# Chunks 2 and 3 of normalised x: 32x32 block turns on DVE and placement through DRAM in place of TensorE transposes

## The chip, the cores and the metric

The kernel runs on one core of one Trainium2 chip. The metric is the device time in microseconds (us) of one execution; lower is better. The engines are named as in the profile: PE (TensorE; PEld is its weight load), DVE (VectorE), ACT (ScalarE), POOL (GpSimd) and SP (SyncE, which here issues nearly all DMA transfers; SPq is its queue of issues).

## What is computed

One transformer-like block on 2048 tokens of width 576, in float32: layer norm without gain or bias, 32-head attention (head width 18), a bilinear GLU of width 4608, and a gated sum.

```python
xn = _layernorm(x, axis=-1)                    # x: [1, 2048, 576]
s = _A_ref(xn, A_wqkv, A_wo)                   # attention, 32 heads, output projection
g = _silu(_B_ref(xn, B_w_gate, B_w_up, B_w_down))   # ((xn @ w_gate) * (xn @ w_up)) @ w_down
return x + s * g
```

The three attention products q, k, v are xn @ wqkv with wqkv of [576, 1728].

## The kernel before

Every float32 product is computed as three products of split operands: a value is written as a high part (float32r, made by an ACT copy) and a low part (the difference, made by DVE or POOL). For normalised x the two parts lie in a tile `xc` of [128, 9, 512] for a chunk of 512 tokens: columns of x (576 of them) on the partitions, tokens along the free axis; slots 0 to 3 hold the high parts of columns 0 to 511, slots 4 to 7 their low parts, slot 8 the last 64 columns, high in partitions 0 to 63 and low in 64 to 127.

There are four chunks of 512 tokens (c = 0 to 3). The kernel has a prologue (about the first 195 us), which makes the columns of x and the q, k and v projections, and a main part, in which a planner interleaves attention with the GLU. The change lies in the prologue, whose order is written out by hand (L557 to L643) and kept on every engine as written.

What one chunk goes through in the prologue:

- `load_x` (L346) brings 512 rows of x into `xin` [128, 4, 576], four transfers of 128 rows, row on partition. There are two such buffers.
- `norm` (L378) runs `norm_stats` (DVE bn_stats twice and bn_aggr, then a square root on ACT, L360) and `norm_apply` (DVE reciprocal, DVE (x - mean) * r into `xn`, L369, and a copy of the last 64 columns beside themselves, L374 on DVE, so that the fifth transpose fills 128 partitions). It is called for two 128-row groups at a time. `xn` has one buffer.
- `to_columns` (L386) turns `xn` with PE: 20 transposes of 128x128 into five PSUM banks (L401). ACT copies each bank into the high slot (L404, L408), DVE subtracts for the low slot (L405, L409). Chunk 0 has its own form, `first_columns`.
- `qk_block` (L458) computes 128 of the 1152 columns of q and k for the chunk's 512 tokens: 14 matmuls of 128x128 by 128x512 (L463) in a bank that is taken in turn from four ("a" and "b", two each). ACT and DVE split the result into `hl` (L466, L467; three buffers), and SP stores it to `sqk` in DRAM (L473; 512 KB in one or two transfers).
- `x_store` (L538) stores `xc` of chunks 1 to 3 to `sx` in DRAM, for the GLU.
- `v_block` (L515) computes v for 128 tokens: two groups of 14 matmuls of 128x128 by 128x288 (L520), in two of the four "g" banks; ACT empties them (L526), SP stores the rows to `sv` (L528). `v_fetch` and `v_split` (L495, L504) load and split the weights of v, in two halves.
- `w_fetch` (L535) loads weights of q and k for two blocks, six transfers (L111, L114).

The loop over chunks:

```python
    for c in range(NCH):
        if c + 2 < NCH:
            load_x(c + 2)
        for b in range(3):
            qk_block(b, c)
        ...
        if c + 1 < NCH:
            to_columns(c + 1)
        for b in range(3, 6):
            qk_block(b, c)
        ...
            if b < 5 and c + 2 < NCH:
                norm(c + 2, (0, 1) if b == 3 else (2, 3))
            if c in (1, 2):
                x_store(c, range(3 * (b - 3), 3 * (b - 2)))
```

So chunk c + 1 is turned between blocks 2 and 3 of chunk c, and chunk c + 2 is normalised while blocks 3 to 5 of chunk c run. With c = 1 there follow, before chunk 2's first block, `w_fetch(3)` and the four v blocks of chunk 0 (called v0 to v3 below), then `w_fetch(4)`. With c = 0 the second half of v's weights is fetched after block 5 (L587).

Each engine works through its instructions in the order in which this code emits them, and so does SP with its DMA issues: an issue whose data is not ready holds back all issues behind it. SP's transfers use eight semaphores in turn, and an issue also waits until the transfer eight before it has landed.

Functions that the diff touches, and what calls them:

Of the kernel before, what the change touches and what calls it, by code (L numbers as in the profile page):

```python
# [20 lines left out]
FT = mybir.dt.float32  # L21
FR = mybir.dt.float32r
I32 = mybir.dt.int32
AF = mybir.ActivationFunctionType
OP = mybir.AluOpType
# [16 lines left out]
def kernel(  # L42
# [10 lines left out]
    nc = tc.nc  # L53
    _, S, D = x.shape
# [5 lines left out]
    NCH = S // 512  # L60
# [6 lines left out]
    dram = ctx.enter_context(tc.tile_pool(name="dram", bufs=1, space=bass.MemoryType.DRAM))  # L67
    consts = ctx.enter_context(tc.tile_pool(name="consts", bufs=1))
    wpool = ctx.enter_context(tc.tile_pool(name="wpool", bufs=1))
    xcp = ctx.enter_context(tc.tile_pool(name="xcp", bufs=2))  # L70
# [6 lines left out]
    sv = dram.tile([S, H, DH + 1], FT, name="sv")  # L77
    sot = dram.tile([D, S], FT, name="sot")
    sg = dram.tile([S, D], FT, name="sg")
    swo = dram.tile([128, 10, D], FT, name="swo")  # L80

    turns = [0]

    def bank(tag, bufs, k=None):
        if tag == "g":
            if k is None:
                k = turns[0] = (turns[0] + 1) % 4
            return psum.tile([128, 512], FT, name="pg", tag=f"g{k}", bufs=1)
        return psum.tile([128, 512], FT, name="p" + tag, tag=tag, bufs=bufs)
# [6 lines left out]
    x2 = x.rearrange("o s d -> (o s) d")  # L96
# [10 lines left out]
    def w_load(srcs):  # L107

        raw = wpool.tile([128, 2, 5, 128], FT, name="wraw", bufs=2)[:, 0:len(srcs)]
        for i, (m, c0) in enumerate(srcs):  # L110
            nc.sync.dma_start(raw[:, i, 0:4, :],  # L111
                              m[0:512, c0:c0 + 128].rearrange("(k p) c -> p k c", p=128))
            for b in (0, 64):
                nc.sync.dma_start(raw[b:b + 64, i, 4, :], m[512:576, c0:c0 + 128])  # L114
        return raw
# [108 lines left out]
    graw, gw, draw, dw = {}, {}, {}, {}  # L224
# [100 lines left out]
    xcs = [None] * NCH  # L325
    vstack, pro = ExitStack(), ExitStack()
    vp = vstack.enter_context(tc.tile_pool(name="vp", bufs=1))
    pp = pro.enter_context(tc.tile_pool(name="pro", bufs=1))
# [15 lines left out]
    xin, xns = {}, {}  # L344

    def load_x(c):  # L346
        xin[c] = ep.tile([128, 4, D], FT, name="xin", bufs=2)
        for t in range(4):
            nc.sync.dma_start(xin[c][:, t, :], x2[c * 512 + t * 128:c * 512 + t * 128 + 128, :])

# [2 lines left out]
    def norm_stats(c, t):  # L353
        st = ep.tile([128, 2, 6], FT, name="st", bufs=4)
        mv = ep.tile([128, 2], FT, name="mv", bufs=4)
        rs = ep.tile([128, 2], FT, name="rs", bufs=4)
        for g in range(2):
            nc.vector.bn_stats(st[:, g, :], xin[c][:, t, g * HALF:(g + 1) * HALF])  # L358
        nc.vector.bn_aggr(mv, st)
        nc.scalar.activation(rs[:, 0:1], mv[:, 1:2], AF.Sqrt, bias=eps)  # L360
        stat[c, t] = mv, rs

    def norm_apply(c, t):
        if t == 0:
            xns[c] = ep.tile([128, 4, 640], FT, name="xn", bufs=1)
        xn = xns[c]
        mv, rs = stat.pop((c, t))
        nc.vector.reciprocal(rs[:, 1:2], rs[:, 0:1])
        op = nc.vector.tensor_scalar(xn[:, t, 0:D], xin[c][:, t, :], mv[:, 0:1], rs[:, 1:2],  # L369
                                     op0=OP.subtract, op1=OP.mult)  # L370
        if c < 2 and t == 3:
            behind.append(op)
        if c:
            nc.vector.tensor_copy(xn[:, t, D:640], xn[:, t, 512:D])  # L374
        else:
            nc.scalar.activation(xn[:, t, D:640], xn[:, t, 512:D], AF.Copy)

    def norm(c, ts=range(4)):  # L378
        for t in ts:
            norm_stats(c, t)  # L380
        for t in ts:
            norm_apply(c, t)

    nqk = [0]

    def to_columns(c):  # L386

        xn = xns.pop(c)
        if c < 2:
            xc = pp.tile([128, 9, 512], FR, name="xcx", bufs=2)  # L390
        else:
            xc = xcp.tile([128, 9, 512], FR, name="xc")
        xcs[c] = xc
        for k in range(5):
            if k < 4:
                p = bank("g", 3)
            else:
                p = bank("a" if nqk[0] % 2 else "b", 2)
                nqk[0] += 1
            for t in range(4):  # L400
                nc.tensor.transpose(p[:, t * 128:(t + 1) * 128],  # L401
                                    xn[:, t, k * 128:(k + 1) * 128], ident)
            if k < 4:
                nc.scalar.activation(xc[:, k, :], p, AF.Copy)  # L404
                nc.vector.tensor_tensor(xc[:, 4 + k, :], p, xc[:, k, :].bitcast(FT),  # L405
                                        op=OP.subtract)
            else:
                nc.scalar.activation(xc[:, 8, :], p, AF.Copy)  # L408
                nc.vector.tensor_tensor(xc[64:128, 8, :], p[64:128, :],  # L409
                                        xc[64:128, 8, :].bitcast(FT), op=OP.subtract)  # L410

    def first_columns():
# [15 lines left out]
        norm_stats(0, 0)  # L428
        norm_stats(0, 1)
        norm_apply(0, 0)  # L430
        norm_stats(0, 2)
        turn(0)
        warm(2)
        wq[0], todo = w_split(raws[0], 2)
        for f, a in todo[:2]:
            f(*a, rest=False)
        norm_apply(0, 1)
        norm_stats(0, 3)
        turn(1)
# [18 lines left out]
    def qk_block(b, c):  # L458
        w, ninth = (t[:, b % 2] for t in wq[b // 2])
        p = bank("a" if nqk[0] % 2 else "b", 2)  # L460
        nqk[0] += 1
        for n, (a, e) in enumerate(QK_PAIRS):
            nc.tensor.matmul(p, w[:, a, :] if a < 9 else ninth, xcs[c][:, e, :], start=n == 0,  # L463
                             stop=n == len(QK_PAIRS) - 1)
        hl = pp.tile([128, 2, 512], FR, name="hl", bufs=3)
        nc.scalar.activation(hl[:, 0, :], p, AF.Copy)  # L466
        nc.vector.tensor_tensor(hl[:, 1, :], p, hl[:, 0, :].bitcast(FT), op=OP.subtract)  # L467
        g0 = blocks[b]
        for kind in range(2):
            lo, hi = max(g0, kind * D), min(g0 + 128, (kind + 1) * D)  # L470
            if lo < hi:
                dst = sqk[kind, :, lo - kind * D:hi - kind * D, c * 512:(c + 1) * 512]
                nc.sync.dma_start(dst.rearrange("h r s -> r h s"), hl[lo - g0:hi - g0].bitcast(FT))  # L473
# [41 lines left out]
    def v_block(t):  # L515
        c, r = divmod(t, 4)
        ps = [bank("g", 3), bank("g", 3)]
        for h in range(2):
            for n, (a, e) in enumerate(PAIRS):
                nc.tensor.matmul(ps[h][:, 0:HALF], xcs[c][:, e, r * 128:(r + 1) * 128],  # L520
                                 vbox["w"][:, a, h * HALF:(h + 1) * HALF], start=n == 0,
                                 stop=n == len(PAIRS) - 1)
        v = vrows[vturn[0] % len(vrows)]
        vturn[0] += 1
        for h in range(2):
            nc.scalar.activation(v[:, 16 * h:16 * h + 16, 0:DH],  # L526
                                 ps[h][:, 0:HALF].rearrange("p (a b) -> p a b", b=DH), AF.Copy)
        nc.sync.dma_start(sv[t * 128:(t + 1) * 128], v)  # L528

    def w_now(i):  # L530
        wq[i], todo = w_split(raws[i], 1 if i == 4 else 2, ep if i == 2 else pp if i == 4 else None)
        for f, a in todo:
            f(*a)

    def w_fetch(i):  # L535
        raws[i] = w_load([(wqkv, b) for b in blocks[2 * i:2 * i + 2]])
# [19 lines left out]

    raws = {}  # L557
    load_x(0)
    w_fetch(0)
    load_x(1)  # L560
    w_fetch(1)
    first_columns()
# [4 lines left out]
# [4 lines that stand above are left out]
            qk_block(b, c)  # L571
            if c == 0 and b == 0:
                w_now(2)
        if c + 1 < NCH:
            to_columns(c + 1)
        for b in range(3, 6):
            qk_block(b, c)
            if c == 1 and b == 3:
                v_split(c)
            if b < 5 and c + 2 < NCH:  # L580
                norm(c + 2, (0, 1) if b == 3 else (2, 3))
            if c in (1, 2):
                x_store(c, range(3 * (b - 3), 3 * (b - 2)))
            if c == 0 and b == 3:
                v_split(c)
            if c == 0 and b == 5:
                v_fetch(1)  # L587
            if c == NCH - 1 and b == 3:
                w_now(3)
        if c == 1:  # L590
            w_fetch(3)
            for t in range(4):
                v_block(t)
            w_fetch(4)
        if c == 2:
            w_now(4)
# [780 lines left out]
    with ExitStack() as end:  # L1377
# [45 lines left out]
        for i, t in enumerate(order):  # L1423
# [13 lines left out]
            y = ys[i % 4]  # L1437
# [3 lines left out]
            xt = xi.pop(t)  # L1441
# [40 lines left out]
```

## Time and profile before

| | |
|---|---|
| time, median of 3 runs (lowest to highest) | 2592.74 us (2592.35 to 2594.34) |
| time of the profiled execution | 2593.44 us |
| its span, first to last instruction | 2591.3 us |
| granted TensorE clock | 1.000 |
| PE busy | 2582.0 us |
| DVE, ACT, POOL busy | 1813.5, 1550.6, 675.8 us |
| PE transposes of `to_columns` (L401) | 60 of 271 to 273 ns, from 21.5 to 82.0 us |
| first matmul of chunk 2's block 0 | 70.34 us |

The page gives the busy time of each engine, the chain of work that ended last (followed back from the last instruction to what released it), and the costliest groups of instructions. The timeline lists instructions in order of time, neighbours of one line merged: start, length, engine, line, operation, tiles, count, and in brackets how long the engine had been idle and for whom. A matmul's end is modelled and neighbours overlap, so the time from start to start is what one costs. DMA issues stand in the rows of SPq; how long a transfer took to land is seen in the chain of waits, where it has a row of its own.

### The profile page before, as it was taken

The numbers are of one execution on the slowest core, as the hardware profiler recorded it, in microseconds if no ns is written. First come the engines' busy times: TensorE is split into PE (matmuls) and PEld (weight loads), VectorE is DVE, ScalarE is ACT, GpSimd is POOL, SyncE is SP. The second block draws the span as 40 slices with busy tenths as digits, with TensorE's granted clock in tenths as the row PEclk, the third lists the DMA queues.
The fourth block names the chain that finished last, engine by engine and source line by source line (L and its number), as shares of the span: only waits on it lengthen the run. The fifth ranks groups of instructions, "written<-read, shape, count | busy, mean of one in ns | idle before, by whom it ended". The sixth has DMA issues, their size and how long they took to land.

```text
span 2591.3 us, 59623 instructions
## 1 busy us (share of the span) xinstructions
PE 2582.0 (100%) x24440; PEld 2132.3 (82%) x24440; DVE 1813.5 (70%) x2996; ACT 1550.6 (60%) x3096; POOL 675.8 (26%) x697
## 2 busy tenths in 40 slices
PE   9999999999999999999999999999999999999999
PEld 7899877888888888888878887777887877877889
DVE  7209777777777778777777877777777777777238
ACT  4223677766766666666666666666666666666621
POOL 3114444434431222222111222111111222221016
PEclk9999999999999999999999999999999999999999
DMA  7899767677653444454444443444444444443357
GB/s 243 251 299 260 202 184 194 184 193 212 175 190 114 142 163 135 151 161 160 142 168 149 142 140 127 138 145 159 121 158 124 145 150 141 133 140 112 124 204 252
DMA packets 186066, 435.65 MB, mean 168 GB/s; under 512 B 51041, under 2 KB 111105, under 8 KB 155585
## 3 DMA queue, kind: packets, MB, share of 16 engines
q1 hardware_dynamic: 183632, 423.88, 53.0%
q0 software_dynamic: 2160, 7.96, 0.8%
q8 instruction: 192, 3.15, 0.5%
q14 instruction: 82, 0.66, 0.1%
HBM read 315.16 MB, written 111.35 MB: 165 GB/s over the span
## 4 chain that ended last, share of the span: by engine, by line
PE 97%; DVE 1%; DMA 1%; ACT 0%; issue 0%; SPq 0%; ACTq 0%; DVEq 0%
PE pg L775 36%; PE pg L734 17%; PE pg L836 16%; PE pa L671 11%; PE pb L723 9%; PE pg L520 2%; PE pb L463 2%; PE pa L463 1%; PE pg L1431 1%; DMA sqk<-hl 1%; PE pb L1431 1%; PE pa L1431 1%; DVE st L358 0%; DMA wgu<-swg 0%; DVE xn L369 0%; PE pa L723 0%
## 5 line engine op out<-in xcount | busy, mean ns | idle before, releaser
L673 DVE TENSOR_REDUCE mx<-pa 128x1 f32<-128x512 f32 x2016 | 1348.8, 687 | 331.9 <-PE pa L671 156.3
L775 PE MATMUL pg<-xc,wgu 64*128 64x512 f32 x7776 | 1442.5, 392 | 0.4 <-DMA wgu<-swg 0.3
L725 ACT ACTIVATE pt<-pb 128x512 f32<-128x512 f32 x2005 | 1144.5, 602 | 471.3 <-PE pb L723 369.0
L775 PEld LDWEIGHTS pg<-xc,wgu 64*128 64x128 f32 x7776 | 1078.8, 186 | 45.5 <-issue 0.8
L836 PE MATMUL pg<-wd,hs 64*128 64x288 f32 x6816 | 877.7, 293 | 0.0
L836 PEld LDWEIGHTS pg<-wd,hs 64*128 64x128 f32 x6816 | 815.2, 185 | 11.6 <-issue 0.8
L671 PE MATMUL pa<-whole,turning 54*128 54x512 f32 x1999 | 783.2, 399 | 0.3 <-DVE mx L673 0.3
L723 PE MATMUL pb<-whole,turning 56*128 56x512 f32 x1978 | 775.2, 398 | 0.0
L734 PE MATMUL pg<-pt,vt 128*32 128x512 f32 x4096 | 453.3, 594 | 0.1
L671 PEld LDWEIGHTS pa<-whole,turning 54*128 54x128 f32 x1999 | 363.3, 184 | 75.3 <-issue 53.0
L816 POOL TENSOR_TENSOR hs<-us,hs 128x512 fp32r<-128x512 f32 x144 | 186.0, 1292 | 866.4 <-ACT hs L800 610.0
L863 POOL TENSOR_TENSOR acc<-acc,st 128x288 f32<-128x288 f32 x284 | 229.5, 810 | 606.0 <-ACT st L893 341.0
L723 PEld LDWEIGHTS pb<-whole,turning 56*128 56x128 f32 x1978 | 360.0, 184 | 5.7 <-ACT pt L725 0.2
L734 PEld LDWEIGHTS pg<-pt,vt 128*32 128x32 f32 x4096 | 126.2, 110 | 285.1 <-issue 279.2
L740 DVE TENSOR_TENSOR oc<-oc,pg 128x512 f32<-128x512 f32 x35 | 24.1, 688 | 221.2 <-PE pg L734 214.9
L257 POOL TENSOR_TENSOR wgu<-wraw,wgu 128x384 fp32r<-128x384 f32 x108 | 108.1, 1014 | 215.3 <-ACT wgu L256 97.6
L738 ACT ACTIVATE oc<-pg 128x512 f32<-128x512 f32 x32 | 19.1, 598 | 229.4 <-PE pg L734 222.0
L899 DVE TENSOR_TENSOR acc<-acc,pg 128x288 f32<-128x288 f32 x261 | 116.3, 448 | 38.5 <-PE pg L836 34.5
L792 DVE TENSOR_TENSOR us<-pg,us 128x512 f32<-128x512 f32 x144 | 98.6, 685 | 54.0 <-PE pg L775 50.9
L893 ACT ACTIVATE st<-pg 128x288 f32<-128x288 f32 x284 | 117.1, 413 | 27.0 <-PE pg L836 19.9
L785 ACT ACTIVATE us<-pg 128x512 f32<-128x512 f32 x143 | 85.5, 598 | 76.6 <-PE pg L775 65.4
L800 ACT ACTIVATE hs<-us 128x512 fp32r<-128x512 f32 x142 | 89.4, 630 | 15.9 <-DVE us L792 15.4
(154 smaller groups left out, 1288.8 us busy)
## 6 DMA issues: line engine op xcount, KB each, us to landing
wgu<-swg SPq DMA_DIRECT2D x102, 1152.0 KB
wd<-swd SPq DMA_DIRECT2D x50, 1152.0 KB
swg<-wgu SPq DMA_DIRECT2D x36, 1152.0 KB
whole<-sqk SPq DMA_DIRECT2D x192, 144.0 KB
turning<-sqk SPq DMA_DIRECT2D x384, 72.0 KB
swd<-wd SPq DMA_DIRECT2D x18, 1152.0 KB
sqk<-hl SPq DMA_DIRECT2D x32, 512.0 KB
xc<-sx SPq DMA_DIRECT2D x24, 512.0 KB
```

Source lines behind the costliest of these rows:

```text
L257: nc.gpsimd.tensor_tensor(w[:, 9 + b:12 + b, :], raw[:, b:b + 3, :], w[:, b:b + 3, :].bitcast(FT), op=OP.subtract)
L671: nc.tensor.matmul(p, q[rows, t * 128:(t + 1) * 128], k[rows, c * 512:(c + 1) * 512], start=True, stop=True)
L673: nc.vector.tensor_reduce(mx[h][:, t, c:c + 1], p, axis=AX.X, op=OP.max)
L723: nc.tensor.matmul(p, k[rows, t * 128:(t + 1) * 128], q[rows, c * 512:(c + 1) * 512], start=True, stop=True)
L725: nc.scalar.activation(pt[t, c // 2][:, c % 2, :], p, AF.Exp, scale=scale)
L734: nc.tensor.matmul(p[32 * c:32 * c + 32, :], vt[h // 2][:, t, 6 * (h % 2):6 * (h % 2) + 32], pt[t, c // 2][:, c % 2, :], start=t == ts[0], ...
L775: nc.tensor.matmul(ps, gw[n][half[r], a, :], xg[i][half[r], e, :], start=k == 0, stop=k == len(TERMS) - 1)
L816: nc.gpsimd.tensor_tensor(hj[:, 1, :], h32, hj[:, 0, :].bitcast(FT), op=OP.subtract)
L836: op = nc.tensor.matmul(ps[:, 0:HALF], hs[u][half[r], j, a, s * 128:(s + 1) * 128], dw[u][half[r], j, e, i * HALF:(i + 1) * HALF], start=( ...
L863: nc.gpsimd.tensor_tensor(a, a, st, op=OP.add)
L893: nc.scalar.activation(st, ps[:, 0:HALF], AF.Copy)
L899: nc.vector.tensor_tensor(a, a, ps[:, 0:HALF], op=OP.add)
```

## The change

For c = 2 and 3, `load_x` places the rows differently (token 128a + 32t + j of a chunk on partition 32a + j, slot t; four transfers that reach 32 partitions each). Once the chunk is normalised, `turn_blocks` turns `xn` in 32x32 blocks on DVE, four instructions of 128x576, back into the `xin` buffer. `blocks_out` stores this with four transfers (pieces of 512 bytes) to a new scratch tensor `sxt` in DRAM, where it lies as columns by tokens. `blocks_in` reads it back with three transfers (pieces of 2048 bytes; 1024 KB and two of 128 KB) into two tiles that use the places of `wd` and `draw`. `late_columns` splits it from SBUF: five ACT copies and five DVE subtractions, as in `to_columns`, which is now called for chunk 1 alone. The copy of the last 64 columns in `norm_apply` goes for chunks 2 and 3. Places in the order: `turn_blocks` right behind the second half of `norm`; for chunk 2 `blocks_out` where the transposes were (c = 1, behind block 2), `blocks_in` behind v0, `late_columns` behind v1; for chunk 3 `blocks_out` behind v1, `blocks_in` behind v3, `late_columns` where the transposes were (c = 2, behind block 2).

```diff
@@ -77,6 +77,7 @@
     sv = dram.tile([S, H, DH + 1], FT, name="sv")
     sot = dram.tile([D, S], FT, name="sot")
     sg = dram.tile([S, D], FT, name="sg")
+    sxt = dram.tile([2, D, 4, 128], FT, name="sxt")
     swo = dram.tile([128, 10, D], FT, name="swo")
 
     turns = [0]
@@ -345,6 +346,11 @@
 
     def load_x(c):
         xin[c] = ep.tile([128, 4, D], FT, name="xin", bufs=2)
+        if c > 1:
+            for a in range(4):
+                r0 = c * 512 + a * 128
+                nc.sync.dma_start(xin[c][32 * a:32 * a + 32], x2[r0:r0 + 128, :].rearrange("(t j) d -> j t d", j=32))
+            return
         for t in range(4):
             nc.sync.dma_start(xin[c][:, t, :], x2[c * 512 + t * 128:c * 512 + t * 128 + 128, :])
 
@@ -370,9 +376,9 @@
                                      op0=OP.subtract, op1=OP.mult)
         if c < 2 and t == 3:
             behind.append(op)
-        if c:
+        if c == 1:
             nc.vector.tensor_copy(xn[:, t, D:640], xn[:, t, 512:D])
-        else:
+        elif c == 0:
             nc.scalar.activation(xn[:, t, D:640], xn[:, t, 512:D], AF.Copy)
 
     def norm(c, ts=range(4)):
@@ -382,14 +388,48 @@
             norm_apply(c, t)
 
     nqk = [0]
+    xraw = {}
+
+    def turn_blocks(c):
+
+        xn = xns.pop(c)
+        y = xin.pop(c).rearrange("p t d -> p (t d)").rearrange("p (b t j) -> p b t j", b=18, t=4)
+        for t in range(4):
+            nc.vector.transpose(y[:, :, t, :], xn[:, t, 0:D].rearrange("p (b j) -> p b j", j=32))
+        xraw[c] = y
+
+    def blocks_out(c):
+
+        y = xraw.pop(c)
+        for a in range(4):
+            nc.sync.dma_start(sxt[c - 2, :, a, :].rearrange("(b i) q -> i b q", i=32),
+                              y[32 * a:32 * a + 32].rearrange("p b t j -> p b (t j)"))
+
+    def blocks_in(c):
+
+        main = wpool.tile([128, 4, 512], FT, name="xt", tag="wd", bufs=1)
+        rest = wpool.tile([128, 512], FT, name="xr", tag="draw", bufs=1)
+        xraw[c] = main, rest
+        xt = sxt[c - 2].rearrange("d a q -> d (a q)")
+        nc.sync.dma_start(main, xt[0:512, :].rearrange("(k p) s -> p k s", p=128))
+        for b in (0, 64):
+            nc.sync.dma_start(rest[b:b + 64, :], xt[512:D, :])
+
+    def late_columns(c):
+
+        main, rest = xraw.pop(c)
+        xc = xcs[c] = xcp.tile([128, 9, 512], FR, name="xc")
+        for k in range(4):
+            x = main[:, k]
+            nc.scalar.activation(xc[:, k, :], x, AF.Copy)
+            nc.vector.tensor_tensor(xc[:, 4 + k, :], x, xc[:, k, :].bitcast(FT), op=OP.subtract)
+        nc.scalar.activation(xc[:, 8, :], rest, AF.Copy)
+        nc.vector.tensor_tensor(xc[64:128, 8, :], rest[64:128], xc[64:128, 8, :].bitcast(FT), op=OP.subtract)
 
     def to_columns(c):
 
         xn = xns.pop(c)
-        if c < 2:
-            xc = pp.tile([128, 9, 512], FR, name="xcx", bufs=2)
-        else:
-            xc = xcp.tile([128, 9, 512], FR, name="xc")
+        xc = pp.tile([128, 9, 512], FR, name="xcx", bufs=2)
         xcs[c] = xc
         for k in range(5):
             if k < 4:
@@ -571,14 +611,20 @@
             qk_block(b, c)
             if c == 0 and b == 0:
                 w_now(2)
-        if c + 1 < NCH:
-            to_columns(c + 1)
+        if c == 0:
+            to_columns(1)
+        elif c == 1:
+            blocks_out(2)
+        elif c == 2:
+            late_columns(3)
         for b in range(3, 6):
             qk_block(b, c)
             if c == 1 and b == 3:
                 v_split(c)
             if b < 5 and c + 2 < NCH:
                 norm(c + 2, (0, 1) if b == 3 else (2, 3))
+                if b == 4:
+                    turn_blocks(c + 2)
             if c in (1, 2):
                 x_store(c, range(3 * (b - 3), 3 * (b - 2)))
             if c == 0 and b == 3:
@@ -591,6 +637,13 @@
             w_fetch(3)
             for t in range(4):
                 v_block(t)
+                if t == 0:
+                    blocks_in(2)
+                if t == 1:
+                    late_columns(2)
+                    blocks_out(3)
+                if t == 3:
+                    blocks_in(3)
             w_fetch(4)
         if c == 2:
             w_now(4)
```

## The prediction

> **What bounds the kernel now.** I read the page first, for the share of PE; then PE's timeline around the transposes, because a shorter PE stream is worth its length only where PE never waits; then SP's and DVE's timelines of the same stretch, because the change puts work there; last the chain of waits.
>
> ```profile
> span 2591.3 us, 59623 instructions
> ...
> PE 2582.0 (100%) x24440; PEld 2132.3 (82%) x24440; DVE 1813.5 (70%) x2996; ACT 1550.6 (60%) x3096; POOL 675.8 (26%) x697
> ...
> PE 97%; DVE 1%; DMA 1%; ACT 0%; issue 0%; SPq 0%; ACTq 0%; DVEq 0%
> ```
>
> PE is the bound from end to end: what it does not do is gained, and what it has to wait is lost, since nothing later has room to give it back. Changes of under 0.2% (5.2 us) cannot be told from none.
>
> ```profile
> 42.95 1.91 PE L401 MATMUL pg<-identr,xn 128*128 128x128 f32 x16
> 44.70 0.60 PE L401 MATMUL pb<-identr,xn 128*128 128x128 f32 x4
> 45.05 3.22 PE L463 MATMUL pa<-xcx,wgu 128*128 128x512 f32 x13
> ...
> 62.80 7.70 PE L520 MATMUL pg<-wv,xcx 128*128 128x288 f32 x56 [0.36 <-ACT vo L526]
> 70.34 3.13 PE L463 MATMUL pb<-xc,wgu 128*128 128x512 f32 x13
> ...
> 79.89 1.91 PE L401 MATMUL pg<-identr,xn 128*128 128x128 f32 x16
> 81.63 0.60 PE L401 MATMUL pa<-identr,xn 128*128 128x128 f32 x4
> 81.99 3.22 PE L463 MATMUL pb<-xc,wgu 128*128 128x512 f32 x13
> ```
>
> The transposes of chunk 2 hold PE from 42.95 to 45.05, those of chunk 3 from 79.89 to 81.99: 2.1 us each, 4.2 in all. That is all that the change can gain, 0.16%. Chunk 2's columns are wanted at 70.34, and PE comes there with a single wait, 0.36 us.
>
> **When the new columns can be there.** `blocks_in(2)` is issued by SP behind the store of v0. SP's order up to that store:
>
> ```profile
> 39.92 0.36 SPq L473 DMA_DIRECT2D sqk<-hl  x1
> 40.38 0.42 SPq L499 DMA_DIRECT2D wvraw<-in_A_wqkv_dram  x1
> ...
> 42.48 2.02 SPq L349 DMA_DIRECT2D xin<-in_A_x_dram  x4
> 45.25 0.38 SPq L473 DMA_DIRECT2D sqk<-hl  x1
> ...
> 64.05 0.37 SPq L473 DMA_DIRECT2D sqk<-hl  x1
> 64.87 1.16 SPq L542 DMA_DIRECT2D sx<-xcx  x2
> ...
> 67.68 0.59 SPq L111 DMA_DIRECT2D wraw<-in_A_wqkv_dram  x1
> ...
> 72.13 3.82 SPq L528 DMA_DIRECT2D sv<-vo  x4
> ```
>
> The store of v0 leaves at 72.13, though v0 was long done: SP works from 64.05 (the store of chunk 1's block 5) through the last four stores of `x_store(1)` and the six fetches of `w_fetch(3)`, 8.1 us of bare issuing. So even with nothing delayed the read-back starts 1.8 us after PE wants its result. This is the main finding; the rest is by how much more.
>
> **What the DVE transposes delay.** They stand in DVE's order ahead of block 5's subtraction, in chunk 0 and again in chunk 1, and block 5's store on SP waits for that.
>
> ```profile
> L747 DVE STREAM_TRANSPOSE od<-oc x32: 697/702/711, 348.5 to 2481.6; 128x512 f32<-128x512 f32 x32
> ...
> 38.19 0.20 DVE L374 COPY xn<-xn 128x64 f32<-128x64 f32 x1
> 38.30 0.16 DVE L368 RECIPROCAL rs<-rs 128x1 f32<-128x1 f32 x1
> ...
> 39.10 0.20 DVE L374 COPY xn<-xn 128x64 f32<-128x64 f32 x1
> 39.21 0.68 DVE L467 TENSOR_TENSOR hl<-pb,hl 128x512 fp32r<-128x512 f32 x1
> ...
> 46.53 2.47 DVE L405 TENSOR_TENSOR xc<-pg,xc 128x512 fp32r<-128x512 f32 x4
> ...
> 57.54 0.68 DVE L374 COPY xn<-xn 128x64 f32<-128x64 f32 x1
> 58.14 0.15 DVE L368 RECIPROCAL rs<-rs 128x1 f32<-128x1 f32 x1
> ...
> 63.34 0.68 DVE L467 TENSOR_TENSOR hl<-pa,hl 128x512 fp32r<-128x512 f32 x1
> ```
>
> One transpose of 128x512 takes 0.70; of 576 elements, in proportion, 0.79. Neighbours overlap: four operations of 0.68 take 2.47, a step of 0.60, so 0.08 less than the length. Four transposes: 4 x 0.71 = 2.8 us. No row shows them with this strided output; as bounds I take this and twice it, and keep the former, because the shape differs little from L747. Two copies go ahead of chunk 0's block 5, 0.11 each (38.19 to 38.30, 39.10 to 39.21), so its subtraction and store come 2.8 - 0.2 = 2.6 later, at 42.5.
>
> What is queued behind that store on SP: `v_fetch(1)`, `load_x(3)` and the store of chunk 1's block 0. And who waits for that one:
>
> ```profile
> 39.92 5.26 DMA sqk<-hl
> 45.25 7.71 DMA sqk<-hl
> 53.06 0.61 ACT hl L466
> ...
> 1057.47 8.25 DMA wgu<-swg
> ```
>
> The block 5 store landed 5.26 after its issue, then the block 0 store left, and landed 7.71 later; only then was an `hl` buffer free and ACT could empty chunk 1's block 3, at 53.06. Behind this on ACT stands `v_split(1)`, behind it on DVE `norm(3)`, then `turn_blocks(3)`, then block 5's subtraction at 63.34. All this moves by 2.6. Off come four copies of chunk 3, one of 0.60 (57.54 to 58.14) and three taken at 0.11, together 0.9; the four transposes add 2.8. The subtraction comes 2.6 - 0.9 + 2.8 = 4.5 later, at 67.8, and the store of v0 at 72.13 + 4.5 = 76.6. PE meanwhile loses its first gain: v0's evictions stand on ACT behind `norm(3)`'s square roots, so v2 starts 2.6 - 0.7 = 1.9 later than 62.80 (two of the copies lie ahead of it), and v3 ends near 72.3. From there PE stands still.
>
> **The read-back.**
>
> ```profile
> 45.00:50.00 5.00, 5.00 (x25) 4.11 (x24) 3.78 (x6) 3.05 (x6) 0.00 (x0) 1.00 1.05 343
> 115.00:120.00 5.00, 5.00 (x24) 4.14 (x23) 1.38 (x2) 0.62 (x2) 0.74 (x2) 1.00 1.12 199
> ...
> 80.58 2.06 ACT L404 ACTIVATE xc<-pg 128x512 fp32r<-128x512 f32 x4
> ...
> 1.46 4.73 PE L336 MATMUL pb<-hl 128*128 128x512 f32 x13 [1.46 <-DVE hl L330]
> 15.15 3.11 PE L463 MATMUL pa<-xcx,wgu 128*128 128x512 f32 x13
> ```
>
> The issue follows 0.5 behind the store (four issues of L349 took 2.02). The 1.05 MB read has no row of its size and pieces. From below, 343 GB/s, the rate of a busy stretch, would give 3.1 us; from above, the 1152 KB read in the chain, 8.25 us, scaled to 1024 KB, gives 7.3. I take the middle, 5.2. Then ACT's first copy, 2.06 / 4 = 0.5. Chunk 2's block 0 starts at 76.6 + 0.5 + 5.2 + 0.5 = 82.8, against 70.34: 12.5 us later, with some 10 us of idle PE.
>
> After its only other long idle time, at the start, PE is slow: 13 matmuls took 4.73 where 13 warm ones take 3.11, 1.6 us more. I add these 1.6; the ACT copies that arrive one per 0.5 us hide in them. Whether an idle stretch in mid-kernel does the same no row shows, so zero is the other end. [...]
>
> The rest costs nothing on the path. `blocks_out(2)` moves 1.18 MB in 512-byte pieces; the stretch from 115 to 120, all 512-byte pieces, shows 199 GB/s, so 5.9 us of transfer around 51 to 60, with 17 us to spare; without that cover it would come on top. `blocks_out(3)` lies in PE's idle time. `blocks_in(3)` waits behind v3's store near 87 and lands by some 93, while its copies stand behind chunk 2's block 2, near 94; short of that, four banks cover 9 us. `late_columns` has the copies and subtractions of before, from SBUF in place of PSUM. For chunk 3 PE saves its 2.1.
>
> Sum: 12.5 + 1.6 - 2.1 = +12.0 us. The profiled execution took 2593.44, 0.7 over the median of 2592.74; against the median, 2604.7.
>
> **Rivals.**
>
> - In time: if SP has the read-back out by 62.0 (PE would want the columns at 70.34 - 2.1 = 68.2, less the 6.2 of issue, read and first copy), PE never waits and saves 4.2: 2592.7 - 4.2 = 2588.5, not slower and within 0.2%. For it speaks that the scratch is long written by then and that v0 ends before; against it the issue rows, which put SP 15 us behind that point.
> - A shorter wait: the first transposes cost nothing, as the block 0 store is held by the landing of others, and PE keeps its clock. Then the delay is 1.9 in place of 4.5, and 12.0 - 2.6 - 1.6 = 7.8: 2600.5. The chain rows speak against the first half.
> - A longer wait, through transfers that reach 32 partitions. If they run at half of the 343 GB/s, the 1.18 MB of `load_x(3)` takes 6.9 in place of 3.4, and all behind it moves by 3.4: 2608. It decides once such a transfer is slower than about 250 GB/s. No row here has a 32-partition transfer. [...]
>
> **How the numbers follow.** Forecast 0.59, in time 0.05, shorter 0.17, longer 0.16, none of these 0.03. Low end: a delay of 1.9, 3.1 for the read, the clock kept: 12.0 - 2.6 - 2.1 - 1.6 = 5.7, 2598.4. High end: transposes twice as long in both places (5.6) and a read of 7.3: 12.0 + 5.6 + 2.1 = 19.7, 2612.5. I give 2598 to 2613. All cases but the first lie over 5.2 us slower; of the unnamed 0.03, 0.02 go to the same and 0.01 to faster: faster 0.01, same 0.07, slower 0.92.
>
> **What would show it.** Right: a gap on PE ahead of chunk 2's block 0, ended by ACT's copy, that one waiting for the read of `sxt`; the store of v0 near 76.6 with the read-back right behind it; block 5's subtractions behind four DVE transposes of 0.8; the first matmuls after the gap slower. Wrong: no gap there; a read-back issued before 70; a gap elsewhere, at v0's second half (waiting for `v_split(1)` on POOL) or ahead of chunk 3; PE at full speed behind the gap.

## The result and the profile after

| | before | after |
|---|---|---|
| median of 4 runs each (lowest to highest) | 2592.86 us (2592.35 to 2594.34) | 2611.0 us (2609.93 to 2612.14) |
| profiled execution: time; span | 2593.44; 2591.3 us | 2612.14; 2610.2 us |

The change makes the kernel slower by 18.1 us: ratio 1.0064, 95% interval 1.0051 to 1.0077. The forecast was 2604.7, 12.0 slower, with a range of 2598 to 2613. (The runs of this table are those taken with the result; each experiment below has its own runs of the kernel before on its own chip, 2593.28 to 2594.47, and its difference is against those.)

The page of the changed kernel: the span; busy time by engine; the chain that ended last, as shares.

```profile
span 2610.2 us, 59572 instructions
...
PE 2585.8 (99%) x24400; PEld 2129.7 (82%) x24400; DVE 1817.7 (70%) x2996; ACT 1552.6 (59%) x3096; POOL 676.1 (26%) x697
...
PE 94%; DMA 2%; DVE 2%; SPq 1%; issue 0%; ACT 0%; DVEq 0%; ACTq 0%
```

40 matmuls are gone (24440 to 24400), and PE's share of the chain fell from 97% to 94%: stretches that PE used to cover are now the wait for something else. PE's busy time even rose by 3.8, although less work is in it, so some of its matmuls got longer. PE's timeline of the changed kernel says where (L503 is the q/k matmul, L463 before; L560 that of v, L520 before):

```profile
44.91 4.83 PE L503 MATMUL pb<-xcx,wgu 128*128 128x512 f32 x13 [1.96 <-DVE hl L507]
...
61.13 3.77 PE L560 MATMUL pg<-wv,xcx 128*128 128x288 f32 x13 [2.78 <-ACT wv L551]
65.26 13.27 PE L560 MATMUL pg<-wv,xcx 128*128 128x288 f32 x85 [0.36 <-POOL wv L552]
88.97 5.30 PE L503 MATMUL pa<-xc,wgu 128*128 128x512 f32 x13 [10.45 <-ACT xc L424]
...
94.33 3.11 PE L503 MATMUL pb<-xc,wgu 128*128 128x512 f32 x13
...
100.68 3.11 PE L503 MATMUL pb<-xc,wgu 128*128 128x512 f32 x13
```

The fourth row is the forecast gap: ahead of chunk 2's block 0 PE is idle for 10.45, ended by ACT's copy of the read-back. That block starts at 88.97 against 70.34 (18.6 later), runs slowly (5.36 to the next block at 94.33, against 3.19 before, from 70.34 to 73.53: 2.2 more), and at block 3 the transposes that are not there any more give 2.1 back: 100.68 against 81.99, 18.7 later. The whole span is 18.9 longer. So all of it happens before 101 us, and nothing later gives it back.

The chain of waits of the changed kernel in the same stretch (start, length, what; DMA rows last from issue to landing):

```profile
22.54 9.19 DMA sqk<-hl
...
42.23 2.05 DVE xin L398 x3
44.28 0.59 DVE hl L507
44.89 5.07 DMA sqk<-hl
50.02 10.02 DMA sqk<-hl
60.15 0.61 ACT hl L506
...
70.08 2.06 DVE xin L398 x3
72.14 0.59 DVE hl L507
...
79.70 0.53 SPq L568
80.27 7.99 DMA xt<-sxt
88.29 0.64 ACT xc L424
88.97 5.52 PE pa L503 x14
```

It is the forecast chain, link by link: the DVE turns (L398) ahead of block 5's subtraction in chunk 0 and again in chunk 1, the store of block 0 between them, v0's store (L568), the read-back right behind it, the first copy. Three links are longer than forecast: the store at 22.54 (7.10 before, not in the sum at all), the store at 50.02 (7.71 before) and the read-back (7.99; forecast 5.2).

### The profile page after: what moved, and what is told of

It reads as the page before. It is cut to its first block, busy times and chain, and to the rows that moved or that the text cites. A ratio compares the mean times of both kernels' runs of the same rounds, so it can differ in the third digit from the quotient of the medians.

```text
span 2610.2 us, 59572 instructions
## 1 busy us (share of the span) xinstructions
PE 2585.8 (99%) x24400; PEld 2129.7 (82%) x24400; DVE 1817.7 (70%) x2996; ACT 1552.6 (59%) x3096; POOL 676.1 (26%) x697
## 4 chain that ended last, share of the span: by engine, by line
PE 94%; DMA 2%; DVE 2%; SPq 1%; issue 0%; ACT 0%; DVEq 0%; ACTq 0%
PE pg L828 36%; PE pg L787 17%; PE pg L889 16%; PE pa L724 11%; PE pb L776 9%; PE pa L503 1%; PE pg L1484 1%; PE pb L503 1%; DMA sqk<-hl 1%; PE pg L560 1%; PE pb L1484 1%; PE pa L1484 1%; SPq L595 1%; DVE st L364 0%; DMA draw<-in_B_w_down_dram 0%
## 5 line engine op out<-in xcount | busy, mean ns | idle before, releaser
L889 PEld LDWEIGHTS pg<-wd,hs 64*128 64x128 f32 x6816 | 815.7, 185 | 11.9 <-issue 0.8
```

The costliest lines, as they stand in the source:

```text
L889: op = nc.tensor.matmul(ps[:, 0:HALF], hs[u][half[r], j, a, s * 128:(s + 1) * 128], dw[u][half[r], j, e, i * HALF:(i + 1) * HALF], start=( ...
```

## The experiments

The theory: the read-back is late because v0's store leaves SP late; what delays that are the DVE turns and the 32-partition loads, and the landing comes on top. The rivals: one of the two alone does it; the scratch stores or the clock make the loss; and, for repairs, that no order of these transfers can do without a wait. The medians have intervals of about 0.09 to 0.17% (2.3 to 4.5 us) to each side, so a difference of a few us between two experiments rests on their timelines more than on their times.

### The loads alone

The kernel before, with only its loads of chunks 2 and 3 changed to 32 partitions each (`b_loads32`):

```diff
+        if c > 1:
+            for a in range(4):
+                src = x2[c * 512:c * 512 + 512, :].rearrange("(t a j) d -> a j t d", t=4, a=4)[a]
+                nc.sync.dma_start(xin[c][32 * a:32 * a + 32], src)
+            return
```

> The kernel before, whose four row loads for each of chunks 2 and 3 bring the same rows to the same places, but in transfers that reach 32 partitions (all four slots) in place of 128 partitions (one slot); nothing else changes. If such transfers are slow (after the change they landed at 221 GB/s where the old ones had 296 and more), the stores queued behind them land later in both places: chunk 0's block 3 is emptied 2.6 us later, chunk 1's block 3 some 5 us later than at 53.06, and PE, which has 0.2 us of room there, waits some 4.5 us at the v blocks: 2597 to 2599. If instead the longer delay after the change came from more transfers being in flight, this kernel has none more and stays at 2593.

2596.03 us, 2.5 more than before (ratio 1.0010, 1.0000 to 1.0019). The rate while `load_x(2)` moves is the plainest evidence of the study. The stretch from 22.5 to 27.5 us (length; busy time and count of PE, PEld, DVE, ACT, POOL; clock; share of the DMA engines; GB/s), first in the kernel before, then in the changed one, then here, then in `a_loads128` below:

```profile
22.50:27.50 5.00, 5.00 (x30) 4.34 (x29) 3.72 (x7) 2.24 (x5) 3.63 (x6) 1.00 0.97 330
```
```profile
22.50:27.50 5.00, 5.00 (x29) 4.29 (x28) 4.29 (x8) 2.04 (x5) 4.21 (x7) 1.00 1.05 217
```
```profile
22.50:27.50 5.00, 5.00 (x29) 4.25 (x28) 3.40 (x6) 1.92 (x4) 3.31 (x6) 1.00 1.04 215
```
```profile
22.50:27.50 5.00, 5.00 (x30) 4.29 (x28) 3.52 (x6) 2.11 (x5) 3.43 (x6) 1.00 1.02 340
```

The DMA engines are busy all the time in all four (shares of 0.97 to 1.05), but move a third less where the loads reach 32 partitions: 217 and 215 GB/s in place of 330 and 340. What lies behind the lower rate no run here shows. What waits is not the load but the q/k store behind it, by the chain of waits of `b_loads32`:

```profile
21.67 8.82 DMA sqk<-hl
...
46.51 8.82 DMA sqk<-hl
55.43 0.61 ACT hl L471
```

8.82 against 7.10, and 8.82 against 7.71; ACT's copy of chunk 1's block 3 comes at 55.43 in place of 53.06. The expectation had 2.6 at chunk 0's block 3 and some 5 here; measured are 1.4 (30.60 for 29.19) and 2.4, and the time is below the 2597 to 2599 expected. PE feels nearly all of the 2.4, in three waits under 1 us and slower matmuls at v0: chunk 2's block 0 starts at 72.66 in place of 70.34.

### The turns alone

The kernel before with four turns per chunk more on DVE, whose result nobody reads (`b_turns`):

```diff
                 norm(c + 2, (0, 1) if b == 3 else (2, 3))
+                if b == 4:
+                    y = xin[c + 2].rearrange("p t d -> p (t d)").rearrange("p (b t j) -> p b t j", b=18, t=4)
+                    for t in range(4):
+                        nc.vector.transpose(y[:, :, t, :], xns[c + 2][:, t, 0:D].rearrange("p (b j) -> p b j", j=32))
```

> The kernel before, with the four DVE block transposes of chunks 2 and 3 added in the places that the change gives them; their result is not used and the PE transposes stay. If DVE's order is on the chain of stores (2.7 us ahead of chunk 0's block 5), chunk 1's block 3 is emptied 2.7 us later and PE waits some 2.5 us at the v blocks: 2595 to 2596. If DVE has room to spare there, 2593.

2596.45, 2.9 more (1.0011, 1.0001 to 1.0020). Block 5's store leaves at 42.84 in place of 39.92, the block 0 store at 47.99 in place of 45.25, and that one lands 7.43 after its issue (7.71 before). So the turns make a store leave later, while the loads make it take longer. Chunk 2's block 0 starts 2.4 later, at 72.75.

### The changed kernel with loads of 128 rows

`a_loads128`: the branch for `c > 1` in `load_x` goes, and `late_columns` undoes the other order of tokens by reading in a permuted order:

```diff
-        if c > 1:
-            for a in range(4):
...
+        own = lambda x: x.rearrange("p (a t j) -> p t a j", a=4, t=4)
+        row = lambda x: x.rearrange("p (t a j) -> p t a j", a=4, t=4)
...
-            x = main[:, k]
-            nc.scalar.activation(xc[:, k, :], x, AF.Copy)
+            x = own(main[:, k])
+            nc.scalar.activation(row(xc[:, k, :]), x, AF.Copy)
```

> The kernel after, with the row loads of chunks 2 and 3 as before the change (128 partitions each); the scratch then holds each chunk's tokens in another order, and the ACT copies and DVE subtractions of the late columns read them in blocks of 32 to put it right. If the 32-partition loads account for the part of the delay that the forecast did not have, the store of v0 goes back from 79.7 to 75 or 76, block 0 of chunk 2 starts 4 to 5 us earlier, and the short waits of PE near 43 and 60 shrink: 2605 to 2607. If they do not matter, 2611.

2607.85, 14.3 more than before (1.0054, 1.0039 to 1.0069), where the change has 18.1, and just above the 2605 to 2607 expected. Its chain of waits is close to the forecast sum:

```profile
42.45 5.09 DMA sqk<-hl
47.61 7.55 DMA sqk<-hl
...
75.00 0.53 SPq L565
75.57 8.12 DMA xt<-sxt
```

Block 5's store at 42.45 (forecast 42.5), the landing of the next 7.55 (7.71 before), v0's store at 75.00 (forecast 76.6). Chunk 2's block 0 starts at 84.39, 4.6 before that of the changed kernel. So the loads cost 4.7 at v0's store (79.70 - 75.00); the read, 8.12 for 5.2, is what is off most.

### The read ahead of block 5

`a_early_read`: `blocks_in(2)` is issued ahead of chunk 1's block 5 in place of behind v0.

```diff
         for b in range(3, 6):
+            if c == 1 and b == 5:
+                blocks_in(2)
             qk_block(b, c)
...
-                if t == 0:
-                    blocks_in(2)
```

> The kernel after, with the three issues that read chunk 2's columns back moved on SP from behind v0's store to ahead of chunk 1's block 5, that is ahead of its store, four stores of x columns and six weight fetches. If the place in SP's order is what made PE wait 10.4 us, the read leaves near 70, lands near 77, the gap ahead of chunk 2's block 0 all but closes and the slow first block (2.2 us) with it: 2598 to 2600. If the transfers themselves were the limit (the scratch not yet written, or the engines full), the gap shrinks by less than half: over 2605.

2604.53, 11.0 more (1.0042, 1.0025 to 1.0059), 7 better than the change, not the 11 to 13 expected. The read left at 69.18, 11.1 earlier, but took 9.06:

```profile
69.18 9.06 DMA xt<-sxt
```
```profile
78.95 6.19 PE L503 MATMUL pa<-xc,wgu 128*128 128x512 f32 x13 [3.45 <-ACT xc L424]
...
121.71 1.20 PE L503 MATMUL pa<-xc,wgu 128*128 128x512 f32 x4 [0.96 <-ACT wgu L130]
```

The gap shrinks from 10.45 to 3.45, the slow block behind it stays, and a wait for weights of q and k appears in chunk 3.

### The turns behind block 5

`a_turn_late`: the turns go behind block 5's subtraction on DVE, so that its store need not wait for them.

```diff
-                if b == 4:
-                    turn_blocks(c + 2)
+            if b == 5 and c + 2 < NCH:
+                turn_blocks(c + 2)
```

> The kernel after, with the DVE transposes of each chunk behind block 5's subtraction instead of ahead of it. By the theory that they hold block 5's store twice (2.7 us each on the chain to v0's store), the store of v0 leaves 5.4 us earlier than at 79.7 and so does chunk 2's block 0: 2605 to 2607. If only the second place counts, because the first is held by the landing of other transfers anyway, 2608 to 2609.

2607.56, 13.7 more (1.0055, 1.0041 to 1.0069). Block 5's store leaves at 40.93, v0's at 74.67, 5.0 before that of the changed kernel; the read takes 8.26. So the turns' place and the loads are worth about the same at v0's store, 5.0 and 4.7. Their sum is more than the 7.6 by which that store is late, so they must overlap; no run has both with the read in its old place.

### All three

`a_all` makes the edits of the three kernels before it together.

> The kernel after with three edits together: the 128-partition loads, the early read of chunk 2 and the DVE transposes behind block 5's subtraction. If these three are the whole cause, PE never waits and the 4.2 us of transposes show: 2588.5 to 2590, just faster than before. If something else holds as well (the extra transfers among the q and k stores), it stays at 2593 or over.

2599.71, 5.9 more (1.0023, 1.0013 to 1.0033): 12 better than the change, and still slower than before. The theory that these three are all of it failed here. The read was issued at 64.61, yet chunk 2's block 0 began only 9.4 later; the gap ahead of it is still there, 5.55, and so is the slow block. PE's timeline:

```profile
74.03 5.75 PE L500 MATMUL pa<-xc,wgu 128*128 128x512 f32 x13 [5.55 <-ACT xc L421]
```

### Are stores behind the read what makes it slow?

`a_out3_late`: chunk 3's scratch stores go from behind v1 to behind v3, so that they cannot be issued while the read runs.

```diff
                 if t == 1:
                     late_columns(2)
-                    blocks_out(3)
                 if t == 3:
+                    blocks_out(3)
                     blocks_in(3)
```

> The kernel after, with the four scratch stores of chunk 3 moved from behind v1 to behind v3, so that they no longer run beside the read of chunk 2's columns. If they are why that read took 8.0 us (chunk 3's took 5.9), it lands 2 us earlier and the whole is 2 us shorter: 2608.5 to 2609.5. If the read is slow by itself, no change: 2611. The read of chunk 3 comes later, which costs nothing unless its copies then come after chunk 2's block 5.

2612.01, 18.2 more (1.0072, 1.0058 to 1.0086): no gain. The read still took 8.44, and during it the DMA engines were neither full nor fast (same columns as above; two halves of the read):

```profile
78.60:82.60 4.00, 0.00 (x0) 0.00 (x0) 0.00 (x0) 0.00 (x0) 0.00 (x0) 0.50 0.69 220
82.60:87.00 4.40, 0.00 (x0) 0.00 (x0) 0.00 (x0) 0.00 (x0) 0.00 (x0) 0.50 0.77 243
```

4.00 us x 220 GB/s and 4.40 x 243 are 1.95 MB. By the sizes of the packets in the trace, 1.30 of this is the read (1.05) with its small companions, 0.41 is v0's store and weight fetches, issued ahead of it, and 0.24 is v1's store, issued behind it. In `a_all` chunk 3's read, behind its own stores, landed in 5.67. Both reads of the changed kernel move under 0.1 MB in their first 2 us, the one of chunk 3 too, which has hardly anything ahead of it; then chunk 2's moves 1.28 MB in 6 us (82.3 to 88.3), chunk 3's 1.23 in 4 (97 to 101). So the queue ahead is not what makes the difference in those first 2 us. Behind them other transfers among the read's take a part; why the rate here was 220 to 243 at a share of 0.69 to 0.77 is open, and the read was not tried with nothing beside it.

### Is the slow block the clock?

`a_warm` keeps PE at work with 40 matmuls of 128x512, whose result nobody reads, behind v3; `a_warm56` has 56 of them.

```diff
                 if t == 3:
                     blocks_in(3)
+                    p = bank("a", 2)
+                    for _ in range(40):
+                        nc.tensor.matmul(p, xcs[0][:, 0, 0:128], xcs[0][:, 0, :], start=True, stop=True)
```

> The kernel after, with 40 extra matmuls of 128x512 (some 9 us, their result unused) behind v3, in PE's idle time ahead of chunk 2's block 0. If the slow first block (5.5 us in place of 3.2) is the clock that drops in idle time, the block runs at 3.2 and the whole is 2 us shorter: 2608 to 2610. If it is the columns arriving one copy at a time, nothing changes: 2611.

> As the earlier run with 40 extra matmuls, which left 5.1 us of idle time behind them and still a slow block; now 56, some 12.7 us, so that under 2 us of idle time stay ahead of chunk 2's block 0. If the clock drops with the length of the idle time, the block runs at 3.2 us and the whole is 2 us shorter than after the change, 2609; if the copies of the columns set its pace, 2611.

With 40: 2612.83, 19.0 more (1.0075, 1.0062 to 1.0089), inconclusive, because they were too few: PE was idle again for 4.7 us and the block was slow again. With 56: 2609.68, 15.2 more (1.0060, 1.0046 to 1.0074); the intervals of this and of the change overlap, but the timelines of PE decide, first with 40, then with 56:

```profile
88.33 5.76 PE L503 MATMUL pa<-xc,wgu 128*128 128x512 f32 x13 [4.69 <-ACT xc L424]
```
```profile
75.84 12.88 PE L649 MATMUL pa<-xcx 128*128 128x512 f32 x56
88.56 3.11 PE L503 MATMUL pa<-xc,wgu 128*128 128x512 f32 x13
```

The same 13 matmuls take 3.11 once PE has not stood still ahead of them, and block 3 starts at 98.08 in place of 100.68. This run alone does not exclude the other explanation: the extra matmuls held PE until 88.56, and ACT's copies, from 85.48 to 88.20, were done by then. The granted clock decides. In the changed kernel it was 0.50 while the slow block ran, up to 93 us, and 0.96 in the microsecond behind it (columns as above):

```profile
89.00:93.00 4.00, 4.00 (x9) 2.82 (x10) 3.14 (x5) 3.20 (x8) 0.00 (x0) 0.50 0.95 263
93.00:94.00 1.00, 1.00 (x6) 0.83 (x5) 0.00 (x0) 0.00 (x0) 0.00 (x0) 0.96 0.98 366
```

Half rate over these 4.0 us loses 2.0, so nearly all of the 2.2 at that block is the clock's. The blocks behind the gaps of 3.45 (`a_early_read`), 4.69 (`a_warm`), 5.55 (`a_all`) and 10.45 took 6.19, 5.76, 5.75 and 5.30; how long PE must stand still for this no run here shows.

### Two rewritten orders

Both have loads of 128 rows and turns behind block 5. `a_best2` rewrites SP's order by hand; `a_pool` lets POOL issue the scratch transfers, out and back.

```diff
+            if c == 1 and b == 4:
+                blocks_in(2)
+            if c == 1 and b == 5:
+                blocks_out(3)
-            if c in (1, 2):
+            if c == 2:
                 x_store(c, range(3 * (b - 3), 3 * (b - 2)))
...
+            x_store(1, range(9))
             w_fetch(4)
```

Of these, `a_pool` keeps the place of `blocks_out(3)` and has `x_store` where it was:

```diff
-            nc.sync.dma_start(sxt[c - 2, :, a, :].rearrange("(b i) q -> i b q", i=32),
+            nc.gpsimd.dma_start(sxt[c - 2, :, a, :].rearrange("(b i) q -> i b q", i=32),
...
+            if c == 1 and b == 3:
+                blocks_in(2)
...
                 if t == 1:
                     late_columns(2)
+                    blocks_in(3)
```

> The kernel after with 128-partition loads, the DVE transposes behind block 5's subtraction, and SP's order rewritten: the read of chunk 2 right behind the store of chunk 1's block 4, the scratch stores of chunk 3 behind block 5's, and the nine slots of chunk 1's x stored behind v3. With the earlier three edits together the read still left at 64.6 and landed at 73.3, 5 us after PE wanted it. If the read's arrival is all that is left, PE has no gap ahead of chunk 2's block 0 and the 4.2 us show: 2589 to 2591. If the q and k stores are then held up by the other transfers, gaps come near 115 and it stays at 2593 or over.

> The same loads and DVE order, but SP's order as after the change without the fourteen transfers of the turned blocks, which POOL issues (chunk 2's read behind its half of v's weights, chunk 3's stores behind block 5, its read behind the late columns of chunk 2). If only the place in SP's queue was in the way, the read lands by 65 and PE does not wait: 2589 to 2591. If POOL's issues are slow or its queue shares the same full DMA engines, a gap stays ahead of chunk 2's block 0: 2593 or over.

2598.18, 3.7 more (1.0015, 1.0006 to 1.0024), and 2597.43, 3.0 more (1.0013, 1.0004 to 1.0022). In both the forecast gap is gone: chunk 2's block 0 starts at 69.03 and 72.61. But other gaps came. PE's timeline of `a_best2`, that of `a_pool`, then the chain of waits of `a_pool`:

```profile
97.56 5.34 PE L500 MATMUL pb<-xc,wgu 128*128 128x512 f32 x13 [5.14 <-DVE hl L504]
```
```profile
57.02 2.81 PE L557 MATMUL pg<-wv,xcx 128*128 128x288 f32 x12 [2.54 <-ACT wv L548]
...
87.40 3.29 PE L500 MATMUL pa<-xc,wq 128*128 128x512 f32 x13 [1.89 <-DVE hl L504]
```
```profile
45.59 10.35 DMA sqk<-hl
...
62.04 8.76 DMA sqk<-hl
```

The releaser is a split into `hl` each time, directly or through ACT's order, and `hl` waits for a q/k store to leave and land. The scratch costs 1.18 MB out and 1.31 MB back per chunk, 5 MB in all, in a stretch in which the q/k stores already decide when `hl` comes free. Taken from one wait, the time turns up in the next.

### What could be gained at all

`b_no_turns`: the kernel before without the 40 transposes and without anything in their place.

```diff
+        if c > 1:
+            for k in range(4):
+                x = xn[:, :, k * 128:k * 128 + 128]
+                hi = xc[:, k, :].rearrange("p (t s) -> p t s", t=4)
...
+                nc.scalar.activation(hi, x, AF.Copy)
...
+            return
```

> The kernel before with the 40 PE transposes of chunks 2 and 3 left out and nothing in their place: the split copies take normalised x from SBUF as it lies, rows on partitions, so the columns of these chunks are not turned and the output differs. It is the ceiling of any version that turns them elsewhere. If PE's stream alone counts, it gains twice 2.1 us: 4.2 less than before. By the theory that v0 waits for the split of v's weights on ACT and POOL, which in the kernel before is there only just in time (PE waits 0.36 at v0), the 2.1 of chunk 2 are lost again in waits at v0's second half and only the 2.1 of chunk 3 are gained: 1.5 to 2.6 less. What tells: waits on PE of about 2 us between 57 and 64 us in the one case, none over 0.5 in the other.

2590.2, 3.1 less than before (0.9989, 0.9980 to 0.9998); the profiled spans differ by 2.4. Its PE timeline:

```profile
57.06 0.40 PE L532 MATMUL pg<-wv,xcx 128*128 128x288 f32 x1 [0.35 <-POOL wv L524]
58.02 4.11 PE L532 MATMUL pg<-wv,xcx 128*128 128x288 f32 x29 [0.56 <-POOL wv L524]
62.60 7.69 PE L532 MATMUL pg<-wv,xcx 128*128 128x288 f32 x56 [0.47 <-ACT vo L538]
70.12 3.13 PE L475 MATMUL pa<-xc,wgu 128*128 128x512 f32 x13
...
79.66 3.11 PE L475 MATMUL pb<-xc,wgu 128*128 128x512 f32 x13
```

Chunk 2's block 0 starts at 70.12, only 0.2 earlier: the 2.1 of chunk 2 are lost again at v0, which now waits for the split of v's weights on POOL (0.35 and 0.56) and for v0's own eviction (0.47), and whose first 26 matmuls take 4.41 from 52.30 on, where 26 of the 56 in 7.59 before would take 3.5. Chunk 3's block 3 at 79.66 in place of 81.99 keeps its 2.1. The interval of the median, 0.5 to 5.2 less, covers both expectations; the timeline decides for the second. So with the rest of the order as it is, the most that turning elsewhere could gain is some 2.3 by the timeline, and the best order found here is 3.0 slower than before.

## Why the prediction was right, and where its sizes were off

The forecast, its sign and its chain were right; the size was 12.0 and is 18.7 by the rows (18.1 by the medians). Term by term:

| term | forecast | measured | from |
|---|---|---|---|
| v0's store later than 72.13 | 4.5 | 7.6 | SPq row at 79.70 |
| issue of the read behind it | 0.5 | 0.6 | 79.70 to 80.27 |
| landing of the read | 5.2 | 8.0 | chain |
| first copy | 0.5 | 0.7 | 88.29 to 88.97 |
| chunk 2's block 0 later than 70.34 (the four, and 1.8 from 70.34 to 72.13) | 12.5 | 18.6 | PE, 88.97 |
| slow clock | 1.6 | 2.2 | 94.33 - 88.97 against 3.19 |
| chunk 3's transposes | -2.1 | -2.1 | 20.8 late at 94.33 (73.53 before), 18.7 at 100.68 |
| sum | 12.0 | 18.7 | |

**The turns** were sized well. DVE's timeline of the changed kernel has four in 2.76, forecast 2.8:

```profile
41.53 2.76 DVE L398 STREAM_TRANSPOSE xin<-xn 128x576 f32<-128x576 f32 x4
44.21 0.65 DVE L507 TENSOR_TENSOR hl<-pb,hl 128x512 fp32r<-128x512 f32 x1
...
69.38 2.76 DVE L398 STREAM_TRANSPOSE xin<-xn 128x576 f32<-128x576 f32 x4
72.06 0.65 DVE L507 TENSOR_TENSOR hl<-pb,hl 128x512 fp32r<-128x512 f32 x1
```

The strided output shows no cost, and the bound of twice the price was not needed.

**The first mis-sized term is v0's store**, and what it lacked is the third rival, which had a chance of its own and was left out of the forecast's sum: loads that reach 32 partitions. Block 5's store of chunk 0 left 5.0 later (44.89), not 2.6, because the q/k store at 22.54 had left 0.6 later and, with `load_x(2)` ahead of it, taken 9.19 for 7.10, which neither the forecast nor the rival had looked at; then the block 0 store took 10.02 for 7.71, because of `load_x(3)`. Those are 2.4 and 2.3; from ACT's copy at 60.15 to the subtraction at 72.06 it is 11.9 against 10.3, 1.6 more where 1.9 was forecast. SP then worked faster through its backlog, 7.0 from block 5's store at 72.74 to v0's in place of 8.1. With the first landing (5.07 for 5.26) it is 5.0 - 0.2 + 2.3 + 1.6 - 1.1 = 7.6. The rival priced it at 3.4 in one place, from an assumed half of 343 GB/s; it was some 2.4 in each of two, at 217 GB/s in the first. `a_loads128` takes it away, and v0's store leaves at 75.00. In `b_loads32`, without the rest of the change, the same loads cost only 1.4 and 1.0; why they cost more beside the turns is open. That answers the shorter wait too: the first turns did delay the block 0 store, by 2.7 in `b_turns`, and nothing absorbed it.

**The second is the read's landing**, 5.2 for 8.0. The middle of two bounds was taken, by the rate of a busy stretch and by a larger read, and neither bound had this read's place in it, among other transfers; the lower one, a rate alone, also left out the first 2 us, in which the reads of the changed kernel move under 0.1 MB. It took 8.0 to 9.1 in the changed kernel and in `a_loads128`, `a_early_read`, `a_turn_late` and `a_out3_late`. The upper bound of 7.3, scaled by size alone, was already too low. What else makes it 8.0 is open.

**The slow clock** is shown by the granted clock of 0.50 and by `a_warm56`, and zero, the other end, is out. The 1.6 was the author's estimate, carried over from the start of the kernel (4.73 for 3.11); it was 0.6 too small.

**In time** did not happen. Its price of 4.2 less was too good as well: `b_no_turns` gains 3.1 by the medians and 2.3 by its timeline, since PE's 2.1 in chunk 2 are not free to take. "All that the change can gain" was a bound on PE's stream, and v0's second half, named as a place where a gap would show the forecast wrong, is where a quicker PE waits. In the changed kernel a wait of 2.78 stands there too, hidden behind the later and longer one.

**Two agreements are chance.** The gap ahead of chunk 2's block 0 was forecast at some 10 us and is 10.45, but both its ends came 6.2 later than forecast. v3 ended at 78.5 in place of 72.3, because PE waited at chunk 1's block 3 and at v0 (1.96 and 2.78) and ran slower behind both (granted clock 0.50 from 46 to 48 and from 63 to 69 us), and block 0 began at 88.97 in place of 82.8. And 2611.0 lies within the range only because its high end had 5.6 for transposes of twice the length, which did not come (without it, 2606.9); the loads and the read took that room.

## What to carry to other kernels

The 4.2 us of work taken off the bound engine here made the kernel 18.1 us longer, because what took its place was not covered: look up which issue the replacement's first transfer stands behind, and add the landing as a busy queue gives it (here 8.0 to 9.1 us for the read of 1.05 MB). In this case the few partitions of a load were a cost of their own, paid by the store queued behind the load (9.19 for 7.10 and 10.02 for 7.71 us); such a cost must be looked for at every place where such a load is issued. Before a move is built for its gain, leave the work out for once and time that.

## What the runs showed that was not expected

- Stores from 32 partitions did not show the low rate of loads to 32 partitions. In the two windows below (columns as above) the changed kernel moved 318 and 310 GB/s, and by the sizes of the packets 0.60 of the 0.63 MB were pieces of 512 bytes, those of `blocks_out(2)`. From 22.5 to 27.5 it moved 217, and 1.04 of the 1.09 MB were pieces of 2304 bytes, those of `load_x(2)`. Why they differ was not tried.

```profile
61.00:62.00 1.00, 0.87 (x3) 0.56 (x3) 1.00 (x3) 1.00 (x5) 0.84 (x2) 1.00 1.06 318
62.00:63.00 1.00, 1.00 (x5) 0.87 (x5) 0.97 (x4) 0.70 (x3) 1.00 (x2) 0.68 1.09 310
```

- Short gaps slowed PE as well: behind a wait of 1.96 us 13 matmuls took 4.83 (at 44.91 in the changed kernel) in place of 3.11, with a granted clock of 0.50 from 46 to 48 us. Behind the wait of 2.78 at 61.13 the clock was 0.50 from 63 to 69 us, and the 13 matmuls of v there took 3.77; behind a wait of 1.58 in `a_turn_late` 13 of them took 3.76. But the length of the wait does not decide it alone: with the waits of 2.54 and 1.89 in `a_pool`, shown above, the mean granted clock of the execution is 1.000, against 0.996 in the changed kernel, and the 13 matmuls behind the second took 3.29. What decides is open.
